# Looping three engines over all eight sets, with two-bank copies and masks, in a decode attention plus gated MLP kernel

## The chip, the cores and the metric

The kernel runs on one core of one Trainium2 chip. The metric is the device time of one execution in microseconds (us); lower is better. A core has a matrix engine (TensorE, "PE", with its weight loads "PEld"), a vector engine (VectorE, "DVE"), an activation engine (ScalarE, "ACT"), a general engine (GpSimd, "POOL") and a synchronization engine (SyncE, "SP") that here issues nearly all DMAs. SBUF is the on-chip working memory with 128 partitions; PSUM holds PE's results in eight banks of 512 fp32 columns. Each engine runs its own instruction list in order; the lists meet at semaphores only.

## The reference

```python
# x [4,1,512]; k_cache, v_cache [4,8,16384,128]; wq [512,4096]; wo [4096,512]
# W_gate, W_up [512,1792]; W_down [1792,512]; all bf16
W = min(4096, max(256, Sk // 4))              # 4096: only the last 4096 keys
q = (x @ wq).reshape(B, Sq, 32, 128).transpose(0, 2, 1, 3)
k = repeat(k_cache[:, :, Sk - W:, :], 4, axis=1)   # 8 K/V heads serve 32 query heads
v = repeat(v_cache[:, :, Sk - W:, :], 4, axis=1)
p = softmax(einsum("bhqd,bhkd->bhqk", q, k) * 128 ** -0.5)
a = einsum("bhqk,bhkd->bhqd", p, v).transpose(0, 2, 1, 3).reshape(B, Sq, 4096) @ wo
gate = x @ W_gate; gate = gate * (gate > 0)
b = (gate * (x @ W_up)) @ W_down
g = sigmoid((x * gate_w).sum(-1, keepdims=True))
out = g * a + (1 - g) * b
```

## The kernel before

The attention is cut into eight **sets**; a set is one batch entry and four of its eight K/V heads (`heads`, L217): 4 MB of K and 4 MB of V. SP issues the loads in a fixed order (L231 to L249, and wq at L568 ahead of all): wq, K0, K1, V0, K2, V1, K3, V2, and so on, then W_gate and W_up into the room of a K set, V7, W_down, and wo in three pieces of 16, 10 and 4 of its 32 row groups with the last two row groups in two halves. K and V have two buffers each (`Ksb`, `Vsb`), so K of set s is issued when the last scores of set s-2 are done (`("SC", s - 2, 3)`, L223), and V of set s when the last values of set s-2 are done (`("PV", s - 2, 3)`, L227). wq and later wo lie in `Wbig`.

The sets' work, by function:

- `kt(s, i)`, L353: K arrives with positions in partitions. PE transposes it as fp32 pairs of bf16, four 128x128 transposes (L363) into one PSUM bank, sixteen times a set (`NFILL`); four banks `TR` take turns. ACT (L368, eleven of sixteen, `ACT_TAKES`) or DVE (L370) copies the bank back to SBUF over the same K.
- `scores(s, bank)`, L373: eight matmuls (L384) of 512 columns fill one of the two banks `SCB`. DVE adds a mask to the bank, writes bf16 scores `sc` and keeps the row maximum (L392), once for each of four banks.
- `maximum(s)`, L396: DVE reduces the four maxima (L398), PE spreads them over partitions (L400, into a `TR` bank), DVE makes the negative maximum (L403).
- `exponent(s, k)`, L409, on ACT and `turn(s, k)`, L416, on DVE: exponential with row sum (L411) and a 32x32 transposition (L418), in two pieces of 1024 columns.
- `values(s, k)`, L421: sixteen matmuls (L429) of the transposed weights with V, four times a set into `OB`; then ACT copies the result (L435).
- `combine(s)`, L438: twelve small fp32 matrix products (L443, L447) gather heads and row sums, DVE divides and multiplies by the gate into `oq` (L450, L451).

The order is software-pipelined: while set s is transposed and scored, set s-1 is exponentiated and multiplied with V (L482 to L515), and set s-2 is combined. Set 0 (L477 to L481) and set 1 are written out; from set 2 on PE runs a hardware loop of three turns with two sets each (`LOOP_FIRST`, `LOOP_TURNS`, `emit`, L134): at the end of a turn it drains and lowers its semaphores by what a turn adds. The instruction lists of DVE and ACT are written out in full. Pool makes the constants at the start (L252 to L287), and copies each set's queries `qS` from `qW` (L343).

After the last set, PE computes gate and up (`gateup`, L455), values and combination of set 7, and then the output in `product` (L529): for each of W_down's 14 and wo's 32 row groups, four matmuls (L530) of 128 columns, one for each of four column groups of PE, all accumulated in one bank. DVE and ACT cast two quarters each (L548, L550), SP writes the result (L574).

Of the kernel before, what the change touches and what calls it, by code (L numbers as in the profile page):

```python
# [5 lines left out]
FP32 = mybir.dt.float32  # L6
# [20 lines left out]
NTR = 4  # L27
NSC = 2
NPIECE = 2
NBANK = 4  # L30
NFILL = 16
WO_CUTS = (0, 16, 26, 30)
ACT_TAKES = (0, 1, 4, 6, 8, 9, 11, 12, 13, 14, 15)
LOOP_FIRST = 2
LOOP_TURNS = 3


class Program:
# [6 lines left out]

    ENGINES = ("pe", "dve", "act", "pool", "sp")

    def __init__(self):
        self.ops = {e: [] for e in self.ENGINES}
        self.events = {}  # L50
        self.counts = {}
        self.history = {}
        self.dmas = []
        self.turns = []
        self.shared = {}

    def op(self, engine, fn, name=None, waits=(), sem=None):
        if name is not None:
            assert name not in self.events, name
            sem = sem or engine  # L60
# [14 lines left out]
    def turn_edge(self):  # L75
        self.turns.append(len(self.ops["pe"]))

    def need(self, engine, waits):
        need = {}
        for w in waits:  # L80
            if w is None:
                continue
            s, n, by, at = self.events[w]
            for own, mine in (("dve", "vd"), ("act", "va")):
                want = mine if engine == "pe" else own
                if by == own and s in (own, mine) and s != want:
                    s = want
                    n = 1 + sum(1 for k in self.history[s] if k < at)
                    assert n <= self.counts[s], w
            need[s] = max(need.get(s, 0), n)  # L90
        return need

    def per_turn(self):

        return self.lowered
# [14 lines left out]
    def signature(self, ops, shift):  # L110
        seen = {}
        out = []
        for fn, name, waits, is_dma in ops:
            here = []
            for s, n in sorted(self.need("pe", waits).items()):
# [7 lines left out]
    def emit(self, engine, eng, sems):  # L123
        ops = self.ops[engine]
        if engine != "pe":
            self.emit_list(eng, sems, engine, ops, {}, {})
            return
        t = self.turns
        self.emit_list(eng, sems, engine, ops[:t[0]], {}, {})
        first = self.signature(ops[t[0]:t[1]], {})  # L130
        for k in range(1, len(t) - 1):
            shift = {s: k * n for s, n in self.lowered.items() if s not in self.shared}
            assert self.signature(ops[t[k]:t[k + 1]], shift) == first, k
        with eng.Fori(0, len(t) - 1):  # L134
            self.emit_list(eng, sems, engine, ops[t[0]:t[1]], {}, {})
            eng.drain()
            for s, n in self.lowered.items():
                eng.sem_inc(sems[s], -n)
        shift = {s: (len(t) - 1) * n for s, n in self.lowered.items() if s not in self.shared}
        self.emit_list(eng, sems, engine, ops[t[-1]:], shift, {})  # L140


def bass_gated_mix__sliding_block_cached__glu_gated_reglu__decode_kernel(
# [13 lines left out]
    with ExitStack() as ctx:  # L157
# [6 lines left out]
        sc = sb("sc", [128, 2, 2048], BF16)  # L164
        pT = sb("pT", [128, 2, 2048], BF16)
        qrow = sb("qrow", [128, 2, 1024], BF16)
        mask = sb("mask", [128, 512], BF16)
# [3 lines left out]
        onesf = sb("onesf", [128, 132], FP32)  # L171
        Wsel = sb("Wsel", [128, 132], FP32)
        Wsum = sb("Wsum", [128, 64], FP32)
        m4 = sb("m4", [128, 20], FP32)
        S32 = sb("S32", [128, 32], FP32)
        xsb = sb("xsb", [5, 512], BF16)
        xT = sb("xT", [128, 4, 32], BF16)
        xw = sb("xw", [5, 512], FP32)
        gwB = sb("gwB", [128, 512], BF16)
        gsb = sb("gsb", [128, 8], FP32)  # L180
        qW = sb("qW", [128, NSET, 2, 32], BF16)
        qS = sb("qS", [128, 2, 2, 32], BF16)
        mx = sb("mx", [128, 2, NBANK], FP32)
        mcol = sb("mcol", [128, 2], FP32)
# [3 lines left out]
        rowsum = sb("rowsum", [128, 2, NPIECE], FP32)  # L188
        osb = sb("osb", [128, 2, 256], FP32)
# [5 lines left out]
        hT = sb("hT", [128, NFT * 4], BF16)  # L195
        outr = sb("outr", [4, 512], BF16)
        banks = [ctx.enter_context(nc.psum_tensor("bank%d" % i, [128, 512], FP32)) for i in range(8)]
        TR = banks[0:NTR]
        SCB = banks[NTR:NTR + NSC]
        OB = banks[6]  # L200
        FB = banks[7]
# [5 lines left out]
        Wq3 = Wbig[:, :].rearrange("p (t w) -> p t w", t=4)  # L207
# [4 lines left out]
        def loop_sem(kind, s):  # L212
            if kind == "K" and s >= LOOP_FIRST or kind == "V" and LOOP_FIRST - 1 <= s < NSET - 1:
# [11 lines left out]
        def load_v(s):  # L225
            P.dma("sp", lambda e: e.dma_start(Vsb[:, s % 2, :], heads(A_v_cache, s)), ("V", s),
                  [("PV", s - 2, 3)] if s >= 2 else [], sem=loop_sem("V", s))  # L227
# [15 lines left out]
        for k in range(len(WO_CUTS) - 1):  # L243
            lo, hi = 512 * WO_CUTS[k], 512 * WO_CUTS[k + 1]
            P.dma("sp", lambda e, lo=lo, hi=hi: e.dma_start(Wbig[:, lo:hi], wo_src[:, lo:hi]), ("WO", k), [("Q",)])
        wo_src3 = A_wo.rearrange("(p i) w -> p i w", p=128)
        for u in range(2):
            P.dma("sp", lambda e, u=u: e.dma_start(Wo3[:, WO_CUTS[-1]:32, 256 * u:256 * u + 256],
                                                   wo_src3[:, WO_CUTS[-1]:32, 256 * u:256 * u + 256]), ("WOL", u), [("Q",)])  # L249


        P.op("pool", lambda e: e.memset(ones[:, :], 1.0), ("ONES",))  # L252
        P.op("pool", lambda e: e.memset(onesf[:, :], 1.0), ("ONESF",))
        P.op("pool", lambda e: e.affine_select(identw[:, :], onesf[:, 0:128], [[-1, 128]], ALU.is_equal, 0.0,
                                               base=0, channel_multiplier=1), ("IDENTW",), [("ONESF",)])
        P.op("pool", lambda e: e.affine_select(ident[:, :], ones[:, :], [[-1, 128]], ALU.is_equal, 0.0,
                                               base=0, channel_multiplier=1), ("IDENT",), [("ONES",)])
        P.op("pool", lambda e: e.memset(xw[:, :], 0.0), ("XW0",))
        P.op("pool", lambda e: e.memset(xT[:, :, :].rearrange("p t r -> p (t r)"), 0.0))
        P.op("pool", lambda e: e.memset(qW[:, :, :, :].rearrange("p s h w -> p (s h w)"), 0.0), ("QZ",))  # L260
# [359 lines left out]
```

## Time and profile before

| quantity | value |
|---|---|
| median of 3 runs | 196.29 us (196.18 to 196.36) |
| profiled execution, its own time | 196.17 us |
| its span in the profile | 194.9 us (1.3 us lie around it) |
| busy: PE, DVE, ACT, POOL | 139.4, 77.2, 76.1, 9.5 us |
| moved by DMA | 81.16 MB, mean 416 GB/s over the span |
| mean granted PE clock | 0.889 |

Busy time is the time in which an engine worked on at least one instruction; the rest of the span it waited. In the lines shown below, a row of the timeline or of the chain begins with the start in us from the span's start and the length in us; `x32` is how many instructions the row holds; what stands in brackets is the engine's idle time before the row and what ended it. Rows of windows give the window, its length, each engine's busy time and number of instructions, the granted clock, the share of the sixteen DMA engines and GB/s.

### The profile page before, as it was taken

The numbers are of one execution on the slowest core, as the hardware profiler recorded it, in microseconds if no ns is written. First come the engines' busy times: TensorE is split into PE (matmuls) and PEld (weight loads), VectorE is DVE, ScalarE is ACT, GpSimd is POOL, SyncE is SP. The second block draws the span as 40 slices with busy tenths as digits, with TensorE's granted clock in tenths as the row PEclk, the third lists the DMA queues.
The fourth block names the chain that finished last, engine by engine and source line by source line (L and its number), as shares of the span: only waits on it lengthen the run. The fifth ranks groups of instructions, "written<-read, shape, count | busy, mean of one in ns | idle before, by whom it ended". The sixth has DMA issues, their size and how long they took to land.

```text
span 194.9 us, 3931 instructions
## 1 busy us (share of the span) xinstructions
PE 139.4 (72%) x1728; PEld 103.6 (53%) x1728; DVE 77.2 (40%) x169; ACT 76.1 (39%) x140; POOL 9.5 (5%) x41
## 2 busy tenths in 40 slices
PE   0135399688789818996898189995995899643834
PEld 0112397366468517763685177854773777422633
DVE  0100045477268302762583026623952456280101
ACT  2005136494285404462854043445641545240001
POOL 8700000000000000000000000000000000000000
PEclk9999999999999995899999855799999579995855
DMA  6999999999999999999999999999999999998993
GB/s 216 444 437 430 430 444 434 430 430 430 440 430 417 437 427 430 437 437 427 430 430 444 430 437 430 430 430 430 430 430 430 430 386 427 479 430 381 429 397 102
DMA packets 3884, 81.16 MB, mean 416 GB/s; under 512 B 409, under 2 KB 930, under 8 KB 1058
## 3 DMA queue, kind: packets, MB, share of 16 engines
q1 hardware_dynamic: 3864, 81.01, 97.3%
q8 instruction: 8, 0.13, 0.3%
q14 instruction: 2, 0.02, 0.0%
q10 hardware_dynamic: 10, 0.01, 0.0%
HBM read 81.01 MB, written 0.00 MB: 416 GB/s over the span
## 4 chain that ended last, share of the span: by engine, by line
DMA 55%; PE 36%; ACT 4%; DVE 3%; issue 1%; SPq 1%; DVEq 0%
DMA Ksb<-in_A_k_cache_dram 43%; PE bank L363 23%; DMA Wbig<-in_A_wo_dram 11%; PE bank L384 6%; ACT Ksb L368 3%; PE bank L429 2%; PE bank L443 2%; DVE Ksb L370 1%; PE bank L530 1%; ACT L411 1%; ACT sc L411 1%; DVE pT L418 1%; PE bank L447 0%; DVE sc L392 0%; PE bank L400 0%
## 5 line engine op out<-in xcount | busy, mean ns | idle before, releaser
L363 PE MATMUL bank<-identw,Ksb 128*128 128x128 f32 x512 | 77.0, 307 | 20.8 <-DMA Ksb<-in_A_k_cache_dram 14.9
L363 PEld LDWEIGHTS bank<-identw,Ksb 128*128 128x128 f32 x512 | 65.3, 158 | 31.6 <-DMA Ksb<-in_A_k_cache_dram 15.8
L368 ACT COPY Ksb<-bank 128x512 f32<-128x512 f32 x88 | 48.7, 589 | 73.0 <-PE bank L363 73.0
L370 DVE COPY Ksb<-bank 128x512 f32<-128x512 f32 x40 | 27.3, 684 | 40.6 <-PE bank L363 40.6
L392 DVE CUSTOM_DVE_ANT_0 sc<-bank,mask 128x512 bf16<-128x512 f32 x32 | 21.8, 682 | 28.8 <-PE bank L384 28.8
L429 PE MATMUL bank<-Vsb,pT 128*32 128x256 bf16 x512 | 20.9, 291 | 6.1 <-DMA Vsb<-in_A_v_cache_dram 6.1
L384 PE MATMUL bank<-Ksb,qS 128*32 128x512 bf16 x256 | 21.0, 405 | 1.8 <-ACT Ksb L368 0.9
L418 DVE STREAM_TRANSPOSE pT<-sc 128x1024 bf16<-128x1024 bf16 x16 | 19.7, 1236 | 2.1 <-ACT sc L411 2.0
L429 PEld LDWEIGHTS bank<-Vsb,pT 128*32 128x32 bf16 x512 | 13.3, 101 | 12.6 <-issue 8.8
L411 ACT ACTIVATE sc<-sc,negmax 128x1024 bf16<-128x1024 bf16 x16 | 18.4, 1151 | 1.9 <-DVE negmax L403 1.8
L443 PEld LDWEIGHTS bank<-osb,Wsel 128*64 128x64 f32 x128 | 9.4, 157 | 4.8 <-issue 3.7
L443 PE MATMUL bank<-osb,Wsel 128*64 128x32 f32 x128 | 10.3, 239 | 0.5 <-ACT osb L435 0.5
L435 ACT COPY osb<-bank 128x256 f32<-128x256 f32 x8 | 3.0, 373 | 17.6 <-PE bank L429 17.6
L400 PE MATMUL bank<-identw,mcol 128*128 128x128 f32 x16 | 3.8, 320 | 7.8 <-DVE mcol L398 4.7
L384 PEld LDWEIGHTS bank<-Ksb,qS 128*32 128x32 bf16 x256 | 4.1, 95 | 9.0 <-ACT Ksb L368 5.7
L400 PEld LDWEIGHTS bank<-identw,mcol 128*128 128x128 f32 x16 | 2.4, 187 | 10.2 <-DVE mcol L398 8.4
L343 POOL COPY qS<-qW 128x64 bf16<-128x64 bf16 x8 | 1.8, 238 | 120.5 <-PE bank L384 110.8
L530 PE MATMUL bank<-Wbig,oq 128*4 128x128 bf16 x128 | 4.2, 307 | 3.8 <-DMA Wbig<-in_A_wo_dram 3.8
L296 PE MATMUL bank<-identw,xw 5*128 5x5 f32 x4 | 0.6, 263 | 8.6 <-DVE xw L290 8.6
L450 DVE RECIPROCAL recip<-bank 64x1 f32<-64x1 f32 x8 | 1.3, 159 | 11.4 <-PE bank L447 11.4
L530 PEld LDWEIGHTS bank<-Wbig,oq 128*4 128x4 bf16 x128 | 3.1, 118 | 4.8 <-DMA Wbig<-in_A_wo_dram 4.7
L314 PE MATMUL bank<-Wbig,xT 128*32 128x512 bf16 x32 | 3.6, 631 | 2.7 <-DMA Wbig<-in_A_wq_dram 2.7
(55 smaller groups left out, 45.4 us busy)
## 6 DMA issues: line engine op xcount, KB each, us to landing
Ksb<-in_A_k_cache_dram SPq DMA_DIRECT2D x8, 4096.0 KB, 21.8
Vsb<-in_A_v_cache_dram SPq DMA_DIRECT2D x8, 4096.0 KB, 30.9
Wbig<-in_A_wq_dram SPq DMA_DIRECT2D x1, 4096.0 KB, 12.2
Wbig<-in_A_wo_dram SPq DMA_DIRECT2D x1, 2048.0 KB, 19.5
Ksb<-in_B_W_gate_dram SPq DMA_DIRECT2D x1, 1792.0 KB, 17.1
Ksb<-in_B_W_up_dram SPq DMA_DIRECT2D x1, 1792.0 KB, 21.0
Vsb<-in_B_W_down_dram SPq DMA_DIRECT2D x1, 1792.0 KB, 15.0
Wbig<-in_A_wo_dram SPq DMA_DIRECT2D x1, 1280.0 KB, 22.1
```

Of the source, the lines that this page charges most:

```text
L314: P.op("pe", lambda e, half=half, t=t, g=g, col=col: e.matmul(SCB[half][32 * g:32 * g + 32, 0:512], xT[:, t, :], Wq3[:, t, col:col + 512], ...
L363: P.op("pe", lambda e, bk=bk, cc=cc, c=c, s=s: e.transpose(bk[:, cc * 128:(cc + 1) * 128], Kw[:, s % 2, c * 128:(c + 1) * 128], identw[:, :]),
L368: P.op("act", lambda e: e.copy(dst, bk[:, :]), ("KTC", s, i), [("KT", s, i)], sem="va")
L370: P.op("dve", lambda e: e.tensor_copy(dst, bk[:, :]), ("KTC", s, i), [("KT", s, i)], sem="vd")
L384: P.op("pe", lambda e, a=a, o=o: e.matmul(bk[32 * a:32 * a + 32, 0:512], qS[:, s % 2, o, :], k4[:, 16 * bank:16 * bank + 16, 32 * a:32 * a ...
L392: P.op("dve", lambda e: e.tensor_tensor_reduce(sc[:, s % 2, bank * 512:(bank + 1) * 512], bk[:, :], mask[:, :], 1.0, LOWEST, ALU.add, ALU.max,
L400: P.op("pe", lambda e: e.matmul(TR[NTR - 1][:, 0:128], mcol[:, par:par + 1].to_broadcast([128, 128]), identw[:, :], start=True, stop=True) ...
L411: P.op("act", lambda e: e.activation(sc[:, par, k * PW:(k + 1) * PW], sc[:, par, k * PW:(k + 1) * PW], ACTF.Exp, bias=negmax[:, par:par + ...
L418: P.op("dve", lambda e: e.transpose(pT[:, par, k * PW:(k + 1) * PW], sc[:, par, k * PW:(k + 1) * PW]), ("PTT", s, k), [("EXP", s, k), ("PV ...
L429: P.op("pe", lambda e, c=c, g=g, blk=blk: e.matmul(OB[32 * g:32 * g + 32, 0:256], pT[:, par, 32 * blk:32 * blk + 32], Vsb[:, par, 256 * bl ...
L443: P.op("pe", lambda e, k=k, lo=lo: e.matmul(FB[r, 384:416], Wsel[:, lo:lo + 64], osb[:, par, 32 * k:32 * k + 32], start=(k == 0), stop=(k ...
L530: P.op("pe", lambda e: e.matmul(AB[32 * cb:32 * cb + 4, 0:128], stat, mov[:, 128 * cb:128 * cb + 128], start=start, stop=stop, tile_positi ...
```

## The change

The numbers of the sets' functions stay; their grain, their order and the way in which the lists are emitted change.

- **Loops.** PE, DVE and ACT each run a hardware loop of four turns with two sets each, over sets 0 to 7; nothing of the sets is written out ahead of it. Semaphores are kept for each pair of engines (`to=`), and each engine lowers its own at the end of its turn; before the loop it raises those on which it waits for the turn before. In the first turn the previous sets are -1 and -2: `maximum(-1)`, `exponent(-1, ·)`, `turn(-1, ·)`, `values(-1, ·)`, `combine(-2)` and `combine(-1)` run on zeroed or leftover data, and `combine(0)` starts again over their result.
- **Grain.** `NFILL` is 8: eight transposes fill a pair of banks (`TR` is two tiles of 1024 columns), and one copy of 1024 columns takes it back, five of eight on ACT. The two score banks are one tile `SCP`; DVE masks 1024 columns at a time. `maximum` uses the first score bank in place of a `TR` bank.
- **Start.** wq lies in V's second buffer, so V1's load now waits for `values(-1)`. wo's loads wait for nothing but their turn on SP. Pool makes selection matrices and masks from the identity by adds and copies, spreads x, computes part of the gate (exponential on ACT, add on Pool, reciprocal on DVE, in place of a sigmoid), and multiplies each set's queries with a column mask.
- **End.** W_down's 14 row groups and wo's first 16 go through 30 matmuls of 512 columns, each on one of four column groups in turn, into the second score bank. ACT copies the bank to `bulk`; four fp32 products with `S32` add it to the output bank after wo's second piece.

```diff
-NFILL = 16
+NFILL = 8
-ACT_TAKES = (0, 1, 4, 6, 8, 9, 11, 12, 13, 14, 15)
-LOOP_FIRST = 2
-LOOP_TURNS = 3
+BULK_PIECES = 1
+ACT_TAKES = (0, 2, 4, 6, 7)
...
+        for s, n in ahead.items():
+            eng.sem_inc(sems[s], n)
         with eng.Fori(0, len(t) - 1):
-            self.emit_list(eng, sems, engine, ops[t[0]:t[1]], {}, {})
+            self.emit_list(eng, sems, engine, ops[t[0]:t[1]], shift(0), {})
             eng.drain()
-            for s, n in self.lowered.items():
+            for s, n in mine.items():
                 eng.sem_inc(sems[s], -n)
...
-        Wq3 = Wbig[:, :].rearrange("p (t w) -> p t w", t=4)
+        Wq3 = Vsb[:, 1, :].rearrange("p (t w) -> p t w", t=4)
...
             P.dma("sp", lambda e: e.dma_start(Vsb[:, s % 2, :], heads(A_v_cache, s)), ("V", s),
-                  [("PV", s - 2, 3)] if s >= 2 else [], sem=loop_sem("V", s))
+                  [("PV", s - 2, 3)] if s >= 1 else [], sem=loop_sem("V", s))
...
+        init(lambda e: e.memset(zs[:, 1024:], 0.0), ("XW0",))
+        init(lambda e: e.memset(rowsum[:, 0, :], 1.0), ("ROW1",), [("XW0",)])
+        init(lambda e: e.tensor_copy(xwv[:, :, 0:1], xsb[:, :].rearrange("r (k h) -> r k h", h=1)),
+             ("XW",), [("XW0",), ("X",), ("GW",)])
...
+        init(lambda e: e.tensor_tensor(t64[:, :], identw[:, 0:64], identw[:, 64:128], ALU.add), ("T64",), [("IDENTW",)])
+        init(lambda e: e.tensor_tensor(S32[:, :], t64[:, 0:32], t64[:, 32:64], ALU.add), ("S32",), [("T64",)])
+        init(lambda e: e.tensor_copy(Wsel[:, 3:128:4], S32[:, :]), ("WSEL",), [("S32",), ("XW0",)])
...
+        init(lambda e: e.tensor_scalar(
+            mask[:, :].rearrange("p (c j) -> p c j", j=4),
+            m4[:, 8:12].rearrange("p (o j) -> p o j", o=1).to_broadcast([128, 256, 4]),
+            1.0, -NEG, op0=ALU.subtract, op1=ALU.mult), ("MASK",), [("M4",)])
...
+        P.op("act", lambda e: e.activation(ez[:, :], FB[:, 32:36], ACTF.Exp, scale=-1.0), ("EZ",), [("Z",)], to="x")
+        init(lambda e: e.tensor_scalar(ez[:, :], ez[:, :], 1.0, None, op0=ALU.add), ("EZ1",), [("EZ",)])
+        P.op("dve", lambda e: e.reciprocal(gsb[:, 0:4], ez[:, :]), ("G0",), [("EZ1",)], to="x")
+        init(lambda e: e.tensor_scalar(gsb[:, 4:8], gsb[:, 0:4], -1.0, 1.0, op0=ALU.mult, op1=ALU.add), ("G",), [("G0",)])
...
         def kt(s, i):
-            bk = TR[f % NTR]
-            for cc in range(4):
+            bk = TR[i % 2]
+            for cc in range(8):
...
+                    w = [("K", s), ("KTC", s, i - 2) if i >= 2 else ("KTC", s - 1, i - 2 + NFILL)]
...
-            dst = Kw[:, s % 2, i * 512:(i + 1) * 512]
+            dst = Kw[:, s % 2, i * 1024:(i + 1) * 1024]
...
-            P.op("dve", lambda e: e.tensor_tensor_reduce(
-                sc[:, s % 2, bank * 512:(bank + 1) * 512], bk[:, :], mask[:, :], 1.0, LOWEST, ALU.add, ALU.max,
-                mx[:, s % 2, bank:bank + 1]), ("SCC", s, bank), w, sem="dve" if bank == NBANK - 1 else "vd")
+            if bank % 2:
+                P.op("dve", lambda e: e.tensor_tensor_reduce(
+                    sc[:, s % 2, pair * 1024:(pair + 1) * 1024], SCP[:, :], mask[:, :], 1.0, LOWEST, ALU.add, ALU.max,
+                    mx[:, s % 2, pair:pair + 1]), ("SCC", s, pair), [("SC", s, bank)], to="dve" if pair else "pe")
...
+        P.op("pe", None, None, [("IDENTW",), ("WSUM",), ("ROW1",), ("QS", 0)])
+        P.op("dve", None, None, [("WSUM",), ("MASK",), ("XW0",), ("G",)])
+        P.op("act", None, None, [("XW0",)])
+        for s in range(NSET):
+            if s % 2 == 0:
                 P.turn_edge()
             maximum(s - 1)
             kt(s, 0)
             kt(s, 1)
             exponent(s - 1, 0)
             kt(s, 2)
             turn(s - 1, 0)
             exponent(s - 1, 1)
+            scores(s, 0)
+            combine(s - 2)
+            if s + 1 < NSET:
+                queries(s + 1)
+            kt(s, 3)
+            turn(s - 1, 1)
+            kt(s, 4)
+            scores(s, 1)
             kt(s, 5)
             kt(s, 6)
             scores(s, 2)
             values(s - 1, 0)
+            kt(s, 7)
             values(s - 1, 1)
             values(s - 1, 2)
             scores(s, 3)
             values(s - 1, 3)
...
+        for n, (stat, mov, waits) in enumerate(rows):
+            g = n % 4
+            P.op("pe", lambda e, g=g, n=n, stat=stat, mov=mov: e.matmul(
+                DB[32 * g:32 * g + (32 if n < 4 else 4), 0:512], stat, mov, start=(n < 4), stop=(n >= len(rows) - 4),
+                tile_position=(0, 32 * g)), ("BULK",) if n == len(rows) - 1 else None, waits, to="act")
+        P.op("act", lambda e: e.copy(bulk[:, :], DB[:, :]), ("BULKC",), [("BULK",)], to="pe")
+        for k in range(BULK_PIECES, len(WO_CUTS) - 1):
             for i in range(WO_CUTS[k], WO_CUTS[k + 1]):
                 for cb in range(4):
-                    product(oq3[:, :, i], Wo3[:, i, :], cb, False, False, None, [("WO", k), ("OQ", NSET - 1)])
+                    product(oq3[:, :, i], Wo3[:, i, :], cb, i == WO_CUTS[BULK_PIECES], False, None,
+                            [("WO", k), ("OQ", NSET - 1), ("OQP", NSET - 3), ("NEGMAX", NSET - 1)])
+            if k == BULK_PIECES:
+                for cb in range(4):
+                    product(S32[:, 0:4], bulk, cb, False, False, None, [("BULKC",), ("WSUM",)])
```

## The prediction, made before the changed kernel ran

> **What bounds the kernel now.** I read the page's queues first, then the chain that ended last, then the timeline at the start, at the first K sets and at the end.
>
> ```profile
> DMA  6999999999999999999999999999999999998993
> q1 hardware_dynamic: 3864, 81.01, 97.3%
> q8 instruction: 8, 0.13, 0.3%
> 51.03 21.79 DMA Ksb<-in_A_k_cache_dram
> 89.85 21.82 DMA Ksb<-in_A_k_cache_dram
> ```
>
> Sixteen DMA engines carry 81 MB and are at least eight tenths busy in all slices but the first and the last. A K load that takes 21.8 us from issue to landing for 4.2 MB stands behind other loads; PE's large share in the chain of page section 4 is only the time before an issue into a queue that was still full. So the end is: start of the first load, 81 MB at the engines' pace, idle DMA, and what follows the last bytes. Compute matters where it lets the queue run dry, and at the end. The q8 line gives a fourth item: 0.3% of 16 x 194.9 us over 8 packets is 1.2 us each, on one engine of the sixteen, which is then that much late.
>
> ```profile
> 1.50:1.75 0.25, 0.00 (x0) 0.00 (x0) 0.00 (x0) 0.09 (x1) 0.25 (x3) 1.00 0.00 0
> 1.75:2.00 0.25, 0.00 (x0) 0.00 (x0) 0.00 (x0) 0.25 (x1) 0.25 (x2) 1.00 4.06 1065
> 22.72 6.57 PE L363 MATMUL bank<-identw,Ksb 128*128 128x128 f32 x32 [4.50 <-DMA Ksb<-in_A_k_cache_dram]
> 35.68 0.53 SPq L222 DMA_DIRECT2D Ksb<-in_A_k_cache_dram  x1
> 72.87 2.74 PE L363 MATMUL bank<-identw,Ksb 128*128 128x128 f32 x12 [4.12 <-DMA Ksb<-in_A_k_cache_dram]
> 111.72 2.82 PE L363 MATMUL bank<-identw,Ksb 128*128 128x128 f32 x12 [3.89 <-DMA Ksb<-in_A_k_cache_dram]
> ```
>
> The first two are windows (last columns: clock, DMA share, GB/s): SP issued the first load at 0.81, bytes flow from about 1.8, so issue to data takes 1.0 us. The others are the timeline. K0 has landed at 22.72. K3 to K5 is 38.85 us for four loads, 9.71 each. Behind K0 only K1 and V0 are queued, so V0 lands at 22.7 + 19.4 = 42.1 and its last bytes leave about 0.5 us earlier (the last bytes of all flow before 192.5 and PE gets them at 192.82): 41.6. K2, issued at 35.68, has data from 36.7: 4.9 us to spare. Later sets have more: at the end of set s, K(s+1) and V(s) are still queued, so a set may take 29 - 1 us from its K's landing; the longest here (111.72 to the issue at 131.15) took 19.4.
>
> **Set 0, the one place with little cover.** Before, set 0 had no previous set to serve. Now the loop covers it, so it also does the exponentials, transposes, combination and values of a set -1 that does not exist: on ACT two L411 (1.15 + 0.19 us each), on DVE two L418 (1.24), on PE 20 instructions of L443/L447 and 64 of L429, 48 of them ahead of the last scores. And copies and masks have two banks each. From pairs of rows (ACT 256 columns 0.373, 512 0.589; DVE 0.417 and 0.684) a 1024-column copy costs 1.03 us on ACT and 1.23 on DVE, the mask 1.23 + 0.08. PE is slow at first: 32 transposes in 6.57 us, 0.205 each, against 16 in 1.97 (0.123) later.
>
> I walk these through in program order, each engine in order. kt0, kt1, kt2: 24 x 0.205 from 22.7, PE at 27.6. The DVE copy of kt1 ends at 27.4, the transpose of piece 0 at 28.7, so scores 0 follow kt2 at once, 28.6; combine (about 1.8) 30.4; kt3 31.3. Then DVE sets the pace: copy 3 ends 32.7, transpose 1 34.0, mask of the pair 35.3, copy 5 36.5. Scores 2 need copy 5: 37.2; values 0, kt7 to 38.7; ACT copy 7 39.8; values 1 and 2 fit before it; scores 3 end at 40.6. The same walk with the old order and old rows gives 14.0 us for set 2 (measured 53.20 to 67.31, 14.1) and 16.9 for set 3 (72.87 to 89.85, 17.0). So K2 is issued at 40.6 instead of 35.7 and brings data at 41.6 to 42.2 (SP spends 0.53 us issuing): level with the end of V0's bytes at 41.6. Bounds: were PE warm from 26 on, the issue falls at 39.6 and nothing is lost; were it slow until 36, at 42.3, and 1.7 to 2.0 us of DMA are lost. I take **+0.5**, range 0 to 2.0. A gap here is not won back, since DMA is full ever after. V1 now waits for values(-1), 0.6 us behind K2, with K2's 9.7 us ahead of it: nothing.
>
> The Trainium skill, "TensorE: Matmul & The Clock Gate", section "Part 1: The HAM clock gate", says that the array starts at half clock, is released after about one busy window of some 3.4 us, and that the windows run free of the kernel. Here 6.5 us went by before the rate rose; by that rule the moment may differ between executions by a window. Worked out from it, set 0 could end a few us earlier or later than in the walk.
>
> Ahead of the set, Pool makes the masks after x has landed (DVE's use of x came at 8.07). Nine operations like its present ones end near 11.6; the 1024-column mask costs 1.2 us at the rate of the present cast (512 in 0.61) or 8.3 at the rate of L284 (128 in 1.04): 12.8 to 19.9, the gate's three small steps and the first qS (after qW at 18.7) end by 20.9 at most, and MT(-1) by 21.5. K0 lands at 22.72: hidden, with 1.2 us in the worse case.
>
> **Sets 1 to 7.** The walk gives 15.6 us at full clock against 14.0, and 20.0 against 19.1 at the lowest. The loop edge that PE has now shows as 1.0 to 1.6 us ahead of L400; DVE and ACT get one too, at the same time. All below 28: nothing. The sigmoid's table load (1.28) goes: hidden already. WD's load waits on set 6's values and goes out at 167.87 now, 10 us ahead of V7's landing at 178.67; 4 us later costs nothing.
>
> **Tail.**
>
> ```profile
> 190.91 2.30 PE L530 MATMUL bank<-Wbig,oq 128*4 128x128 bf16 x64 [1.25 <-DMA Wbig<-in_A_wo_dram]
> 192.13 0.52 PEld L530 LDWEIGHTS bank<-Wbig,oq 128*4 128x4 bf16 x20 [0.27 <-DMA Wbig<-in_A_wo_dram]
> 192.82 0.10 PEld L530 LDWEIGHTS bank<-Wbig,oq 128*4 128x4 bf16 x4 [0.17 <-DMA Wbig<-in_A_wo_dram]
> 192.98 0.60 DVE L548 CAST outr<-bank 4x128 bf16<-4x128 f32 x2 [8.35 <-PE bank L530]
> ```
>
> Wo's second piece lands at 190.91, the third at 192.13, the last at 192.82, and PE nearly keeps up: 64 products took 1.88 us one piece earlier, 29 ns each, so 40 end at 192.09 and 20 more at 192.72. Only 0.14 us of PE is free. The change moves W_down's rows and Wo's first 16 rows into 30 products of 512 columns; the 16 stream as many columns as the 64 before (done near 189.7), and the ACT copy (0.59) ends at 190.3: hidden by 0.6 us. But the four fp32 products that add this block stand behind the 40 products and ahead of the last 24. An fp32 product is two instructions here (L400: 16 for 8 sets). At this slow clock an fp32 instruction of 128 columns takes 0.235 us (L363, 12 in 2.82), so eight take 1.88 in series; if the four column groups overlap as in L530, a quarter, 0.47. Between the two, 1.0; less 0.14 gives **+0.85**, range 0.3 to 1.75. The casts and the out DMA (192.98 on) follow as before.
>
> The Trainium skill, "FP8 and Floating Point Precision", section "TensorE Precision Notes", says that true fp32 goes through the array in four passes, and "TensorE: Matmul & The Clock Gate", section "Back-to-back issue gap", that a pass of N columns takes N/1.2 ns when cold. An estimate from these is 0.43 us a product, 1.7 for four in series; the sum would be +1.5 here.
>
> **Code.** PE's static program loses two unrolled sets (some 500 instructions) and gets about 160 fewer in the tail. Fewer code packets: those of the first sets stay, one of the last may go. At the end the DMA rate falls over 2 us (281, 183, 35 GB/s from 190 to 193), which is engines finishing unevenly; one packet fewer on the latest is worth at most 1.2. I take **-0.3**, range -1.3 to 0.
>
> **Sum.** +0.5 + 0.85 - 0.3 = +1.05 on the profiled execution's 196.17 us (span 194.9), or 197.2; the median of the runs shown, 196.29, is 0.12 above it, so 197.2 to 197.3. I say 197.2.
>
> **Rivals.**
> - *Hidden anyway* (0.15): PE warms early, K2 is in time, the fp32 products overlap, the code saving pays for them: 0 + 0.33 - 0.3, 196.3. For it: 4.9 us of cover before; against it, the walk uses 4.9 of them.
> - *Faster* (0.12): the latest engine is late only by code packets, and the shorter program takes them off it. Price: up to 1.3 us at the last landing; it decides if set 0 and the tail together cost under 0.9. With +0.4 for the two, 195.4. For it: the uneven finish; against it: any one packet that is left makes its engine late by as much.
> - *Larger loss* (0.13): PE stays at half clock through set 0, as for 12.9 us from 111.72, and the fp32 products run in series: +2.0 + 1.75 - 0.3, 199.7; one of the two alone gives 198.2 to 198.8.
> - That two-bank copies make the steady state slower does not decide: it would take 28 us a set.
>
> **How the numbers follow.** The forecast has 0.60: 196.7 to 198.0. Differences within 0.2%, 0.4 us, can't be told from none here. Range: low end 196.0 to take in "hidden", high end 198.7 to take in one of the two larger costs at its bound. Most of "faster" and the rest of the larger loss stay outside. Faster 0.12, same 0.15, slower 0.73.
>
> **What would show it.** Right: K2's issue near 40.6, a dip of the DMA share between 41 and 43, 24 us or less for every later set, no other dip; eight fp32 instructions between Wo's pieces, and PE rather than DMA last before the casts. Wrong: K2 issued before 40; a dip elsewhere (a set over 28 us); the casts straight behind the last landing.

## The result, and the profile after

The changed kernel takes 198.62 us (median of five executions, 197.82 to 198.71) where the kernel before takes 196.18 beside it: slower, 1.0116 of the time before, 95% interval 1.0096 to 1.0137, or 1.2%. The profiled execution of the changed kernel is its fastest, 197.82 us with a span of 196.6. It is 1.65 us longer than the profiled execution before (196.17), and the median is 2.44 us longer. The forecast was 197.2, about +1.0.

From the page of the changed kernel, the queue and code lines and two steps of its chain (start, length, what):

```profile
DMA  6999999969999999999999999999999989998991
q1 hardware_dynamic: 3864, 81.01, 96.5%
q8 instruction: 5, 0.08, 0.2%
74.61 19.02 DMA Ksb<-in_A_k_cache_dram
94.17 18.89 DMA Ksb<-in_A_k_cache_dram
```

The same 81 MB flow, and one slice of forty, the ninth (39.3 to 44.2 us), has fallen from 9 to 6. (The 33rd shows 8 in place of 9, but its bytes are nearly those of before, 381 GB/s against 386.) Code packets fell from 8 to 5. A K load now takes 19.0 us from issue to landing instead of 21.8, so it is issued with less queued ahead of it, and it goes out straight after the K before has landed (74.61 + 19.02 = 93.63, the next issue at 94.17). Where that comes from is in the next two views: SP's waits (us in total, times, longest) and the timeline from the end of set 0's scores to set 1's first transposes.

```profile
SPq L266 <- PE tr L400: 123.1, 6, 37.6
```

```profile
38.08 0.62 PE L422 MATMUL scp<-Ksb,qS 128*32 128x512 bf16 x8
38.75 1.22 DVE L428 CUSTOM_DVE_ANT_0 zs<-scp,mask 128x1024 bf16<-128x1024 f32 x1 [3.90 <-PE scp L422]
40.02 0.15 DVE L434 TENSOR_REDUCE zs<-zs 128x1 f32<-128x2 f32 x1
40.23 0.49 PE L436 MATMUL scp<-identw,zs 128*128 128x128 f32 x2 [1.09 <-DVE zs L434]
40.55 1.91 PE L400 MATMUL tr<-identw,Ksb 128*128 128x128 f32 x16
40.85 0.53 SPq L266 DMA_DIRECT2D Ksb<-in_A_k_cache_dram  x1
```

The K loads (L266) wait for a transpose (L400), not for scores (L422). Scores 3 of set 0 are done at 38.70; K2 is issued at 40.85, when the mask, the maximum, its spread over PE and the first transpose of set 1 are over: 2.15 us later. What that does to the queue, in windows of the changed kernel (last columns: clock, DMA share, GB/s):

```profile
40.00:41.00 1.00, 0.77 (x7) 0.78 (x8) 0.40 (x3) 0.00 (x0) 0.10 (x1) 1.00 1.23 524
41.00:42.00 1.00, 1.00 (x12) 1.00 (x11) 0.05 (x2) 0.38 (x1) 0.21 (x1) 1.00 0.14 49
42.00:43.00 1.00, 0.77 (x8) 0.53 (x7) 0.50 (x1) 1.00 (x2) 0.00 (x0) 1.00 1.09 360
43.00:44.00 1.00, 1.00 (x12) 0.66 (x13) 0.92 (x2) 0.96 (x3) 0.00 (x0) 1.00 0.39 164
```

By the packets of the trace, V0's bytes are over between 41.3 and 41.6 on fourteen of the sixteen engines; one more, which carried a 16 KB code packet at 41.41, ends at 42.35, and the last at 43.09. K2's packets begin between 42.2 and 43.25, on average 1.2 us behind the end of V0's, and the first one on each engine takes 1.21 to 2.09 us where a later one takes 1.21. Windows of 1 us are coarse here; in twelve us around the place it is 356 GB/s against 429 before (below). The gap stays: the load behind K2 is V1, and its first packet starts at 52.61 against 50.92 before, 1.69 later; the middle of the sixteen engines is 1.6 later. The end of the changed kernel, from its timeline:

```profile
192.27 1.24 PE L565 MATMUL scp<-Wbig,oq 128*4 128x128 bf16 x40 [1.22 <-DMA Wbig<-in_A_wo_dram]
193.19 0.24 PEld L565 LDWEIGHTS scp<-bulk,S 128*4 128x4 f32 x8
193.30 0.64 PE L565 MATMUL scp<-bulk,S 128*4 128x128 f32 x8
193.72 0.92 PE L565 MATMUL scp<-Wbig,oq 128*4 128x128 bf16 x24
194.61 0.59 DVE L594 CAST outr<-scp 4x128 bf16<-4x128 f32 x2 [7.59 <-PE scp L565]
```

wo's second piece lands at 192.27 instead of 190.91 (+1.36), and from there to the first cast it takes 2.34 us instead of 2.07 (+0.27). Together +1.63, nearly the 1.65 of the profiled execution.

### The profile page after: what moved, and what is told of

The parts are those of the page before. It is cut to its first block, busy times and chain, and to the rows that moved or that the text cites. A ratio compares the mean times of both kernels' runs of the same rounds, so it can differ in the third digit from the quotient of the medians.

```text
span 196.6 us, 3919 instructions
## 1 busy us (share of the span) xinstructions
PE 138.3 (70%) x1752; PEld 103.7 (53%) x1752; DVE 79.8 (41%) x127; ACT 70.1 (36%) x97; POOL 14.2 (7%) x34
## 4 chain that ended last, share of the span: by engine, by line
DMA 61%; PE 19%; DVE 13%; ACT 4%; issue 1%; SPq 1%; DVEq 0%
DMA Ksb<-in_A_k_cache_dram 49%; DMA Wbig<-in_A_wo_dram 11%; PE tr L400 10%; DVE Ksb L408 5%; DVE zs L428 5%; PE scp L422 4%; ACT Ksb L406 4%; DVE pT L454 2%; PE fb L479 2%; PE scp L565 1%; PE scp L436 1%; PE ob L465 1%; PE fb L483 0%; DVE zs L434 0%; SPq L289 0%
## 5 line engine op out<-in xcount | busy, mean ns | idle before, releaser
L400 PE MATMUL tr<-identw,Ksb 128*128 128x128 f32 x512 | 70.8, 296 | 7.6 <-DMA Ksb<-in_A_k_cache_dram 6.7
L400 PEld LDWEIGHTS tr<-identw,Ksb 128*128 128x128 f32 x512 | 62.2, 152 | 14.9 <-DMA Ksb<-in_A_k_cache_dram 7.9
L406 ACT COPY Ksb<-tr 128x1024 f32<-128x1024 f32 x40 | 40.5, 1012 | 78.2 <-PE tr L400 78.0
L408 DVE COPY Ksb<-tr 128x1024 f32<-128x1024 f32 x24 | 29.4, 1223 | 29.5 <-PE tr L400 29.5
L428 DVE CUSTOM_DVE_ANT_0 zs<-scp,mask 128x1024 bf16<-128x1024 f32 x16 | 19.3, 1205 | 31.2 <-PE scp L422 31.2
L422 PE MATMUL scp<-Ksb,qS 128*32 128x512 bf16 x256 | 20.0, 387 | 13.0 <-DVE Ksb L408 12.1
L465 PE MATMUL ob<-Vsb,pT 128*32 128x256 bf16 x576 | 21.8, 289 | 7.9 <-DMA Vsb<-in_A_v_cache_dram 7.9
L454 DVE STREAM_TRANSPOSE pT<-zs 128x1024 bf16<-128x1024 bf16 x18 | 22.2, 1238 | 1.8 <-ACT zs L447 1.3
L465 PEld LDWEIGHTS ob<-Vsb,pT 128*32 128x32 bf16 x576 | 15.6, 101 | 13.9 <-issue 9.7
L447 ACT ACTIVATE zs<-zs,negmax 128x1024 bf16<-128x1024 bf16 x18 | 20.7, 1150 | 2.0 <-DVE negmax L439 2.0
L422 PEld LDWEIGHTS scp<-Ksb,qS 128*32 128x32 bf16 x256 | 3.9, 95 | 21.2 <-DVE Ksb L408 18.0
```

The costliest lines, as they stand in the source:

```text
L400: P.op("pe", lambda e, cc=cc, c=c: e.transpose(bk[:, cc * 128:(cc + 1) * 128], Kw[:, s % 2, c * 128:(c + 1) * 128], identw[:, :]), ("KT", ...
L406: P.op("act", lambda e: e.copy(dst, bk[:, :]), ("KTC", s, i), [("KT", s, i)], to="pe")
L408: P.op("dve", lambda e: e.tensor_copy(dst, bk[:, :]), ("KTC", s, i), [("KT", s, i)], to="pe")
L422: P.op("pe", lambda e, a=a, o=o: e.matmul(bk[32 * a:32 * a + 32, 0:512], qS[:, s % 2, 32 * o:32 * o + 32], k4[:, 16 * bank:16 * bank + 16, ...
L428: P.op("dve", lambda e: e.tensor_tensor_reduce(sc[:, s % 2, pair * 1024:(pair + 1) * 1024], SCP[:, :], mask[:, :], 1.0, LOWEST, ALU.add, A ...
L447: P.op("act", lambda e: e.activation(sc[:, par, k * PW:(k + 1) * PW], sc[:, par, k * PW:(k + 1) * PW], ACTF.Exp, bias=negmax[:, par:par + ...
```

## The experiments

All have one row in common, and the table reads best after it: the window from 38 to 50 us, in which the kernel before moves 429 GB/s. "K2" is the time of its issue in the profiled execution. An engine carries about ten packets of 32 KB in such a window, so a row can be off by some per cent. The row of the kernel before:

```profile
38.00:50.00 12.00, 10.18 (x128) 7.23 (x126) 7.46 (x13) 8.78 (x16) 0.00 (x0) 1.00 0.99 429
```

| kernel | K2 issued | GB/s 38–50 | profiled, us | median (lowest to highest), us | ratio to before [95%] |
|---|---|---|---|---|---|
| before | 35.68 | 429 | 196.17 | 196.18 | 1 |
| after | 40.85 | 356 | 197.82 | 198.62 (197.82–198.71) | 1.0116 [1.0096, 1.0137] |
| a1_again | 41.82 | 329 | 198.79 | 198.17 (197.99–198.79) | 1.0096 [1.0081, 1.0111] |
| e1_signal | 39.47 | 384 | 198.05 | 197.61 (196.87–199.60) | 1.0079 [1.0043, 1.0114] |
| e2_before_late | 36.92 | 426 | 196.10 | 196.36 (196.10–196.57) | 1.0004 [0.9995, 1.0013] |
| e3_warm | 39.84 | 389 | 197.13 | 198.06 (197.13–198.22) | 1.0089 [1.0074, 1.0103] |
| e4_bulk_early | 41.38 | 367 | 198.08 | 198.20 (198.08–199.04) | 1.0109 [1.0093, 1.0124] |
| s1_hold2 | 37.92 | 430 | 196.42 | 196.26 (196.10–196.92) | 1.0008 [0.9999, 1.0017] |
| s2_hold4 | 40.37 | 393 | 197.68 | 197.69 (197.53–197.72) | 1.0075 [1.0060, 1.0089] |
| s3_hold7 | 42.00 | 318 | 198.62 | 198.37 (197.75–198.76) | 1.0103 [1.0086, 1.0120] |
| e6_all | 38.77 | 419 | 196.12 | 196.23 (196.10–198.19) | 1.0029 [1.0006, 1.0052] |
| e7_early_wo | 42.70 | 436 | 196.81 | 196.74 (195.96–197.83) | 1.0027 [1.0006, 1.0047] |
| e8_early_wo_signal | 39.36 | 419 | 197.84 | 196.85 (195.94–197.84) | 1.0025 [1.0010, 1.0041] |
| e9_small_wo | 39.85 | 400 | 196.57 | 196.77 (196.12–197.83) | 1.0034 [1.0017, 1.0050] |

After the first result the theory was: the loss is K2's late issue, most of it from the wait that stands in for scores 3, plus a little in the tail. The rivals: PE's slow start in set 0, the fp32 products at the end, or the loops themselves.

**e1_signal: a signal of its own for the K loads.** In the changed kernel, the first matmul of `values(s-1, 3)`, next after scores 3 on PE, signals SP; nothing else is edited.

```diff
-                    ("PV", s, k) if c == 15 and k == 3 else None, w, to="act")
+                    ("PV", s, k) if c == 15 and k == 3 else ("XS", s) if c == 0 and k == 3 else None, w,
+                    to="x" if c == 0 else "act")
```

> The changed kernel, but the first matmul of values(s-1, 3), which PE runs right behind the last scores of set s, raises the semaphore that SP's K loads wait on. Theory A (K2's load is held not by scores 3 of set 0 but by its stand-in, the first transpose of set 1, 2.1 us later; with the longer set 0 this empties the DMA queue): K2 is issued at about 38.8 us instead of 40.85, its data flows before V0's last bytes leave at 41.3, the dip of the DMA share at 41 to 42 goes, and the time falls by 1.4 to 2.2 us to 196.3 to 196.7. Theory B (set 0's dead work is the loss, the wait's place costs little): at most 0.5 us less, 198.1. Theory C (the loss is spread over the sets or lies outside this gap): no change, 198.6.

The wait is gone: K2 goes out at 39.47, right behind scores 3 (39.35 in this execution, in which PE reached full clock later). The time is 197.61, 0.9 us more than hoped. It is 1.0 us below the changed kernel's first median and 0.6 below a1_again's, but its executions spread over 2.7 us and its interval overlaps the changed kernel's, so the gain of the signal alone is not shown. The queue still runs thin, in the profiled execution of e1_signal:

```profile
39.47 0.54 SPq L266 DMA_DIRECT2D Ksb<-in_A_k_cache_dram  x1
```

```profile
41.00:42.00 1.00, 1.00 (x10) 1.00 (x11) 0.30 (x2) 0.00 (x0) 0.00 (x0) 1.00 0.96 311
42.00:43.00 1.00, 1.00 (x11) 0.87 (x8) 0.00 (x0) 0.73 (x1) 0.00 (x0) 1.00 0.82 262
```

Apart from the one engine that V0 holds until 42.97, K2's packets begin between 41.4 and 42.7, 1.9 to 3.2 us after the issue. The low end of that is partly V0's, whose bytes hold the engines until 41.15 to 41.9; the first packets take up to 1.8 us. Two things had been taken for known that were not: that an issue at 39.5 is in time, and that data follows an issue after 1.0 us.

**e2_before_late: the stand-in alone, in the kernel before.** Its K loads wait for the first transposes of the set before as well.

```diff
-                  [("SC", s - 2, NBANK - 1)] if s >= 2 else [], sem=loop_sem("K", s))
+                  [("SC", s - 2, NBANK - 1), ("KT", s - 1, 0)] if s >= 2 else [], sem=loop_sem("K", s))
```

> The kernel before, with every K load from K2 on held also by the first four transposes of the next set, as the stand-in holds it after the change. Theory A: K2 goes out at about 37.5 instead of 35.7, still 3 us ahead of need, and later K loads have 9 us of queue ahead of them: 196.2, no change. Theory D (the stand-in wait alone costs in every set, because a K load then waits for the landing of the K before it): 0.2 us or more in each of six loads, 197.4 or more.

1.0004 [0.9995, 1.0013]: nothing. With the short set 0 of before, the late wait puts K2 at 36.92, still in time, and in sets 1 to 7 it costs nothing. In this kernel the stand-in harms nothing; in the changed one it comes on top of a longer set 0.

**e3_warm: PE at full clock from the start of set 0.** Eight extra matmuls of 512 columns, whose results nobody reads, run on PE ahead of the loop.

```diff
+        for n in range(8):
+            P.op("pe", lambda e: e.matmul(TR[0][:, 0:512], ones[:, :], Wq3[:, 0, 0:512], start=True, stop=True),
+                 None, [("ONES",)])
```

> The changed kernel with eight more 512-column matmuls on PE, whose results nobody reads, between the query transposes (18.1 us) and the loop, so that PE is busy until about 22 us. Theory A: set 0 then starts at full clock, its last scores end near 37.5, the stand-in near 39.6 and K2's data flows from 40.6, ahead of 41.3: no dip, 196.3 to 196.8. If PE's clock in set 0 plays no part, or the matmuls do not raise it: 198.6, or up to 0.5 more, as the loop's first step comes later.

Set 0's first 24 transposes, timeline of e3_warm and then of the changed kernel:

```profile
22.98 1.97 PE L400 MATMUL tr<-identw,Ksb 128*128 128x128 f32 x16 [0.68 <-DMA Ksb<-in_A_k_cache_dram]
25.17 1.09 PE L400 MATMUL tr<-identw,Ksb 128*128 128x128 f32 x8 [0.23 <-ACT Ksb L406]
```

```profile
22.64 4.19 PE L400 MATMUL tr<-identw,Ksb 128*128 128x128 f32 x24 [2.43 <-DMA Ksb<-in_A_k_cache_dram]
```

With the matmuls, scores 3 end at 37.7 and K2 goes out at 39.84, again 2.2 us behind. The profiled execution gains 0.7 us on the changed kernel's, but the median, 198.06, is hardly different from a1_again's 198.17, and 1.3 us above the range expected: a warm PE alone doesn't bring the queue back.

**e4_bulk_early: the fp32 products out of the tail's last stretch.** `BULK_PIECES = 0` adds the block ahead of wo's second piece.

```diff
-BULK_PIECES = 1
+BULK_PIECES = 0
```

> The changed kernel with the 512-column block holding only W_down's 14 row groups, and the four fp32 products standing behind wo's first piece, ahead of its second; wo's first 16 row groups go through 64 products as before the change. Traced theory (eight fp32 instructions took 0.42 us in the tail, the casts start 2.34 us behind the second piece's landing instead of 2.07): 0.2 to 0.4 us less than the changed kernel, 198.2 to 198.4. The prediction's size for it: 0.85 less, 197.8.

From the landing of the second piece to the first cast, timeline of e4_bulk_early:

```profile
192.76 2.35 PE L565 MATMUL scp<-Wbig,oq 128*4 128x128 bf16 x64 [1.37 <-DMA Wbig<-in_A_wo_dram]
194.86 0.59 DVE L594 CAST outr<-scp 4x128 bf16<-4x128 f32 x2 [8.58 <-PE scp L565]
```

2.10 us, against 2.34 in the changed kernel and 2.07 before: the products cost 0.24 there. The whole time doesn't show it, since K2 went out at 41.38 in this execution, 0.53 later.

**s1_hold2, s2_hold4, s3_hold7: the kernel before with K2 alone held back.** Nothing of the change is in them; only the load of K2 also waits for the third, fifth or eighth transposed bank of set 1. This separates the late issue from all else.

```diff
-                  [("SC", s - 2, NBANK - 1)] if s >= 2 else [], sem=loop_sem("K", s))
+                  [("SC", s - 2, NBANK - 1)] + ([("KT", 1, 2)] if s == 2 else []) if s >= 2 else [],
+                  sem=loop_sem("K", s))
```

> The kernel before, with K2's load alone held until set 1's third group of transposes, near 38.4 us. Theory A1 (an issue has data 1.0 us later, as at the start of the kernel): data at 39.4, ahead of V0's end at 41.3: 196.3. Theory A2 (under load it takes 1.4 to 3.5 us to reach all sixteen engines, as the traces of the changed kernel and of its variants show at 40 us): at the edge, 196.3 to 196.8.

> The kernel before, with K2's load alone held until set 1's fifth group of transposes, near 40.3 us. Theory A1: data at 41.3, level with V0's end: 196.3 to 196.6. Theory A2: data at 41.7 to 43 on the different engines: 197.3 to 198.0.

> The kernel before, with K2's load alone held until set 1's eighth group of transposes, near 42.2 us. Theory A1: data at 43.2, 1.9 us late: 198.2. Theory A2: the queue is empty by then, 1.0 to 1.7 us from issue to data, 2 to 2.6 us late: 198.3 to 198.9. If a late K2 is not what costs the time (the changed kernel's loss lies elsewhere): 196.3 in all three.

The windows from 38 to 50 of the three, in this order:

```profile
38.00:50.00 12.00, 10.17 (x128) 7.16 (x132) 7.39 (x13) 8.55 (x15) 0.00 (x0) 1.00 1.01 430
```

```profile
38.00:50.00 12.00, 10.19 (x129) 7.27 (x127) 7.46 (x13) 8.80 (x16) 0.00 (x0) 1.00 0.96 393
```

```profile
38.00:50.00 12.00, 10.06 (x127) 7.05 (x127) 7.46 (x13) 8.75 (x15) 0.00 (x0) 1.00 0.78 318
```

With issues at 37.92, 40.37 and 42.00 in the profiled executions, the medians are 0.03, 1.46 and 2.14 us above 196.23, and the profiled executions themselves 0.19, 1.45 and 2.39. So a late K2 alone makes a loss of the size seen, with the old loops, the old grain and the old tail. It begins between 37.92 and 40.37, and not near 40.6, where the prediction had put it. The changed kernel's row is this one:

```profile
38.00:50.00 12.00, 10.16 (x115) 8.08 (x116) 7.84 (x12) 5.71 (x9) 0.31 (x1) 1.00 0.86 356
```

Its issue at 40.85 lies between the second and the third, and so does its rate.

**e6_all: e1, e3 and e4 in one.**

> The changed kernel with the three edits of before together: the direct signal for K loads, eight more matmuls ahead of the loop, and wo's first piece through 128-column products. Theory A: K2 is issued near 37.6, 3.7 us ahead of V0's end, no dip; the tail is that of the kernel before; fewer code packets: 195.9 to 196.5, level with the kernel before. If something else of the change costs time in the sets or at the start: 197 or more.

K2 goes out at 38.77, the queue stays full, and the second piece's landing and the first cast are back at 190.81 and 192.90 (before: 190.91 and 192.98):

```profile
38.00:50.00 12.00, 10.21 (x116) 8.13 (x117) 7.90 (x12) 5.68 (x8) 0.31 (x1) 1.00 0.98 419
```

Eight of the twelve executions take 196.1 to 196.6, four 197 to 198.2. The median is that of before; the interval of the ratio, 1.0006 to 1.0052, is not, because of those four. In the profiled execution the extra matmuls did not hold PE at full clock: the trace's records show half clock from 23.3 to 26.7 us, and the 24 transposes took 4.51 us, as in e1_signal (4.54). So it is mostly the signal that brought K2 forward here. Loops, two-bank copies and selection matrices therefore cost nothing that shows in most executions once K2 is early. What the four wait for was not profiled.

**a1_again: the changed kernel unedited, beside the last batches.**

> The changed kernel once more, unedited, on the chip that runs the next two. Theory A with the clock: its executions differ in when PE reaches full clock in set 0, so K2's issue falls between 40.8 and 41.5 us and the time between 197.8 and 198.8, later issue with longer time. If the executions differ for another reason: K2's issue near 40.85 beside a time of 198.6.

198.17, and a profiled execution of 198.79 in which K2 went out at 41.82: its first 24 transposes took 5.38 us instead of 4.19.

```profile
22.80 5.38 PE L400 MATMUL tr<-identw,Ksb 128*128 128x128 f32 x24 [2.43 <-DMA Ksb<-in_A_k_cache_dram]
```

By the trace's clock records, full clock was granted from 28.4 us here and from 25.5 in the first profiled execution. K2 0.97 us later goes with a time 0.97 us longer. The kernel before varies by 0.3 to 0.6 us between the executions of a batch; the changed one by 0.8 to 0.9. That this wider spread comes from that clock fits the two profiled executions, and no other execution of it has a trace.

**e7_early_wo: cover instead of speed.** Waits and sets stay as in the changed kernel; twelve of wo's row groups (1.6 MB, some 3.8 us of the engines) are loaded between V0 and K2, into `Wbig`, which is empty since wq moved.

```diff
-WO_CUTS = (0, 16, 26, 30)
+WO_CUTS = (0, 12, 16, 26, 30)
...
+            if s == 2:
+                P.dma("sp", lambda e: e.dma_start(Wbig[:, 0:512 * WO_CUTS[1]], A_wo.rearrange("(p i) w -> p (i w)", p=128)[:, 0:512 * WO_CUTS[1]]),
+                      ("WO", 0))
...
-        for k in range(len(WO_CUTS) - 1):
+        for k in range(1, len(WO_CUTS) - 1):
```

> The changed kernel with the same waits and the same sets, but wo's first 12 row groups (1.6 MB, 3.6 us of DMA) are loaded between V0 and K2 instead of at the end, so that the DMA queue has work until about 45 us; rows 12 to 15 stay in the 128-column products ahead of the last three pieces. Theory A: K2, issued at 40.8 to 41.5, is then 3.5 us or more ahead of need, no dip, and the time is that of the kernel before, 196.0 to 196.5, without touching set 0 or the wait. If set 0's length or the stand-in cost time by another way than the empty queue: 197.5 or more.

K2 is issued at 42.70, the latest of all, and nothing is lost there:

```profile
38.00:50.00 12.00, 10.12 (x138) 7.96 (x140) 5.99 (x11) 6.25 (x9) 0.31 (x1) 1.00 1.02 436
```

This is the other half of the proof: with cover in the queue, the latest issue of all leaves no dip. The median falls by 1.4 us from a1_again beside it, to 196.74. Some 0.5 us remains, and the executions spread from 195.96 to 197.83.

**e8_early_wo_signal: e7 with e1's signal.**

> The kernel of the early wo load with the direct signal for the K loads as well. Theory A: nothing is left for the signal to win, 196.0 to 196.5, within 0.2 us of the kernel with the early wo load alone. If the stand-in still costs something in later sets: 0.3 us or more less than that.

196.85: with cover in the queue the signal wins nothing. The profiled execution, the longest of its twelve, is held by PE at the end, where 64 products stand back to back after the fp32 additions, at 25 ns each against 18 for e7's forty. The granted clock from 190 to 193 us is 0.50 in e8's profiled execution and 1.00 in e7's (timeline of e8_early_wo_signal, then of e7_early_wo):

```profile
192.60 0.61 PE L569 MATMUL scp<-bulk,S 128*4 128x128 f32 x8 [0.25 <-ACT bulk L583]
192.98 1.60 PE L569 MATMUL scp<-Wbig,oq 128*4 128x128 bf16 x64
```

```profile
191.52 0.73 PE L568 MATMUL scp<-Wbig,oq 128*4 128x128 bf16 x40 [0.65 <-DMA Wbig<-in_A_wo_dram]
192.77 1.06 PE L568 MATMUL scp<-Wbig,oq 128*4 128x128 bf16 x24 [0.52 <-DMA Wbig<-in_A_wo_dram]
```

The early piece moves V7, W_down and their products nearer to the end: V7 is there at 182.45 in e8 against 178.67 before, while the last bytes flow at 192.5 against 192.4. So in that execution PE, at half clock, is last, and not DMA. The clock in the tail is thus one cause of e8's spread that the traces show for one execution; over its twelve, the longer ones tend to have the lower mean clock (195.94 at 0.947, 197.84 at 0.896), but e9 below shows no such order.

**e9_small_wo: e8 with four row groups early instead of twelve.**

```diff
-WO_CUTS = (0, 12, 16, 26, 30)
+WO_CUTS = (0, 4, 16, 26, 30)
```

> e8 with the early piece of wo cut from 12 row groups to 4 (0.5 MB, some 1.3 us of the sixteen engines instead of 3.8); signal straight from the values as in e8. Theory (the loss is the empty queue near 41 to 43 us and nothing else that is large): K2's issue near 39 to 40.5, cover for it until about 40.3, so no dip or one under 0.5 us; V7 lands 1.3 instead of 3.8 us later, so W_down's and wo's products are no longer crowded at the end: 196.0 to 196.5 median. Rival (the loops cost the remaining 0.5 us in the tail, whatever the queue does): 196.7 to 197.0 as in e7 and e8.

196.77: the crowded tail was not the remainder either, or a smaller cover gave back what the tail gained (400 GB/s against 419 to 436). In the profiled execution K2 left at 39.85, and its first packets took up to 2.3 us instead of 1.21. The rival's number came out, but not its reason: the time lies again between 196.1 and 197.8 for one and the same program, which is no fixed cost of the loops. In the profiles of e7 and e9 the last bytes of wo reach PE 0.6 and 0.5 us later than before (193.45 and 193.30 against 192.82), about their whole excess; why that is, and why it differs between executions, stays open. No version is shown to beat the kernel before; the lowest executions of e7 and e8, 195.96 and 195.94, are within 0.1 us of its lowest.

## Why the prediction was right and wrong, step by step

The direction, the place (K2, between V0's bytes and its own) and the two costs were the ones that decided. The step that failed is the size of the term for K2. The sum had +0.5 for it, since data was to follow an issue after 1.0 us and so be level with the end of V0's bytes; the data came 1.36 to 2.40 us after the issue, and the gap cost 1.36 us up to wo's second piece in the fastest execution and 2.25 in a1_again. The tail was mis-sized the other way, +0.85 against +0.27.

- *"So K2 is issued at 40.6 instead of 35.7"* came out at 40.85, for the wrong reason. Two errors offset each other. The walk released K2 by scores 3. But scores signal DVE (`to=`), and SP belongs to the group "x"; for a wait on another group's event the new `need()` takes the next signal that the same engine gives to the waiting one's own group:

```diff
+        kind = engine if engine in self.LOOPED else "x"
...
+            if by is not None and s[1] not in (kind, "all"):
+                s = (by, kind)
+                n = 1 + sum(1 for k in self.history[s] if k < at)
```

  PE's next signal to "x" is the first transpose of the next set. The lines were in the diff, and the walk didn't follow them: 2.15 us. The other way, the walk had the end of scores 3 at 40.6, and it was 38.70, since PE reached full clock at 25.5 and not 29. In a1_again, where the clock rose later, the issue is at 41.82. Its own bound for this case, "were PE warm from 26 on", gave 39.6, so 0.9 of the 1.9 us was the walk's and 1.0 the clock's.
- *"issue to data takes 1.0 us"* is the reading that made the term too small. Its window row, 1065 GB/s for a quarter of a microsecond, is 266 KB, or eight packets of 32 KB: the first eight of the sixteen engines. By the packets of that same trace, the sixteen began 1.03 to 1.71 us after the issue, and the first packet of each took 1.4 to 2.1 us instead of 1.21. At K2 it was 1.36 to 2.40 us in the changed kernel and 1.34 to 2.10 in s3_hold7, with first packets as slow. So most of the difference was already in the idle start, on the engines that the row leaves out; the first engine is 0.3 us later at K2 and the last 0.4 to 0.7. K2's data were not level with the end of V0's bytes but 1.2 us behind on average, about 1.5 with the slow first packets. The cover of before was not the 4.9 us of the text: e6_all, issued 3.1 us after the 35.68 of before, shows no dip, and e1_signal, 3.8 us after it, does.
- *V0's last bytes at 41.6*: right for fourteen engines, 41.3 to 41.6. The two late ones, 42.35 and 43.09, were not in it.
- *"A gap here is not won back"*: right in the main. V1's first packet is 1.69 us late and the second wo piece 1.36.
- *The clock gate.* The rows first: the same 24 transposes took 4.19, 4.54 and 5.38 us in the profiled executions of after, e1_signal and a1_again, and 3.28 us from start to end where PE was kept busy before (e3_warm, 22.98 to 26.26). The Trainium skill, "TensorE: Matmul & The Clock Gate", section "Part 1: The HAM clock gate", says that the windows run free of the kernel; the spread between executions agrees. The issues fell inside the walk's bounds of 39.6 and 42.3 (40.85 and 41.82), but what the text says of the early one, that nothing is lost at 39.6, did not hold: e1_signal, at 39.47, has a dip.
- *Tail, +0.85 between 0.3 and 1.75*: +0.27. The eight fp32 instructions are there, between wo's pieces, and PE is last before the casts, as said. But they take 0.64 us, not 1.88: the low end of the two, where the column groups overlap, was right, and the middle was a choice without a row. The estimate from "FP8 and Floating Point Precision" (the Trainium skill, section "TensorE Precision Notes"), 1.7 us for four in series, doesn't apply, since they are not in series here.
- *Code, -0.3*: 5 code packets for 8, as expected in kind. Since +1.36 and +0.27 already account for 1.63 of the 1.65 us in the profiled execution, and the gap of 1.6 to 1.7 shows as 1.36 at the end, some 0.3 may be theirs; no run tells it apart.
- *Sets 1 to 7, nothing*: right. No other slice shows a dip, and e2 shows that the later wait costs nothing there. The cover is smaller than the text's, though, since a K load now waits for the landing of the K before it: when K3 goes out at 58.07, V1 still flows until 62.3, and when K4 goes out at 74.61, V2 until 81.7.
- *Pool's masks hidden*: right. The 1024-column mask took 3.63 us from 12.03, between the two ends of 1.2 and 8.3.
- *The rivals.* "Hidden anyway" would have needed an issue before about 39, which of the changed sets only e6_all reached. "Faster" needed the late engine to be late by code alone. "Larger loss" named +2.0 for K2 with PE at half clock through set 0. A loss of that size came (+2.25 in a1_again), but not for that reason: full clock was granted from 28.4 us, about as in the walk, and the stand-in's 2.2 us and the slower data made up the rest. The tail's 1.75 did not come.

## What to carry to other kernels

When a planner replaces a wait by a later signal that happens to exist, follow the replacement to the event that really releases each transfer; here it moved a load from the end of the scores past four operations on two engines. Count a transfer's lead from data on the engines, not from its issue, and read that delay on the last of the sixteen engines, not on the first. When a load can't be issued in time, something already ready, put ahead of it in the queue (e7), can cover the gap; e7's median is still 0.5 us above the kernel before, for reasons that stay open.

## What the runs showed of the hardware

From the issue of a load to its first packet it took 1.03 to 1.71 us over the sixteen engines at the idle start of the kernel before, and 1.36 to 2.40 us at K2 in the changed kernel, where the queue had just run dry; in both, the first packet of most engines took longer than the 1.21 us of a later one, up to 2.1. A 16 KB code packet took 0.9 to 1.2 us on one engine before and after the change, not much less than a 32 KB data packet (1.21). And between two profiled executions of the changed kernel the full clock was granted 2.9 us apart (25.5 and 28.4 us), which went with K2's issue 0.97 us later.
